# Two token groups share one transposed tile and run their late gate slices together; the sink selection is built by VectorE

## The chip, the cores and the metric

The kernel runs on one core of one Trainium2 chip. A core has TensorE (PE in the profile, with its weight loads shown apart as PEld), VectorE (DVE), ScalarE (ACT), GpSimd (POOL) and SyncE (SP, which here issues DMAs only). The metric is the device time of one execution in microseconds, the median of repeated runs. The profile's own span of one execution (238.3 us) is a little shorter than the device time (240.77 us), since it counts from the first profiled instruction to the last.

## The reference, cut to what matters

Attention with four sink tokens and a window of 128, over 4 batches, 8 heads, 768 positions and head size 64, is followed by a gated feed-forward block over the 3072 tokens it gives:

```python
scores = scale * np.matmul(q, k.transpose(0, 1, 3, 2))
keep = is_sink | in_window            # k < 4, or 0 <= q - k < 128
a = softmax(where(keep, scores, -1e9))
x = (a @ v) with heads joined         # 3072 x 512
g = x @ w_gate                        # 512 x 1536
silu = g * (1.0 / (1.0 + np.exp(-g)))
out = silu * (x @ w_val) @ w_out      # 1536 x 512
```

## The kernel before, in words

**Groups and blocks.** Attention is done in twelve groups of 256 tokens (`g`, three to a batch). The feed-forward block is done in token blocks `tb` of the sizes in `SIZES`: three of 256 tokens (groups 0, 1 and 2), four of 512, and one of 256. For each block the attention output `xn` (tokens on partitions) is transposed into `xT` (model dimension on partitions), in `step_X` (L379): for groups 0, 1, 2 and 4 by TensorE (`px`, L393) and a copy from PSUM (L396 on ScalarE, L400 on VectorE), for the others by a DMA transpose (L388).

**A gate unit.** `gate_a` (L419) projects `xT` with a slice of 128 columns of w_gate into a PSUM bank `pg` (L414) and takes a Tanh on ScalarE into `th` (L428). `gate_b` (L431) projects with w_val into `pv`, and VectorE forms `u = (th + 1) * pg` (L434) and `ht = u * pv` (L435), which is twice the gated value; the factor one half comes with the output copy. A bank holds 512 columns. So for a block of 512 tokens a unit covers one of the twelve slices `f` with four matmuls of 512 columns per projection, and for a block of 256 tokens it covers two slices with eight matmuls of 256 columns. `down` (L453) multiplies `ht` with w_out (L466), 12 matmuls for 128 tokens, copies on ScalarE (L471) and stores through SyncE (L474).

**Order.** Everything is put in order by hand: each engine runs its instructions in the order in which the program lists them, and waits on semaphores where data or a buffer isn't ready. `weave` (L504) goes through a list of units `us` and puts attention steps of later groups into each unit, between its gate projection and its value projection, at the slots given. VectorE work of attention collected in `later` comes after the unit's own `u` and `ht` when `flush` runs. The first list (L634) holds the units of blocks 0 and 1 interleaved (indices 0 to 11), then those of block 2, then the output units of all three. `both` (index 3) starts two units, one of each group, before it finishes either; `alone` (index 2) holds only the transposes of group 1.

**The sinks.** For queries in groups with `c > 0` the four sink keys lie outside the group's own window tiles. Their exponentials `es` (L324) are multiplied with `vsb` (L335), in which a row for each head and sink holds that sink's value in the column block of its head and zero elsewhere. `vsb` for a batch is the sink values (`vcf` for batch 0) times a selection `diag_h` (L270). The selection is made from `th8`, an iota made early (L195): for each of four places q and four heads h, one where `0 <= th8 < 4`, and then joined over q. Before the change GpSimd makes it at L593 to L598 in seven operations: less than, greater or equal, their product, three additions, and a cast. Then GpSimd makes `vsb` for batch 0 (L270) and goes on to issue loads: `nat` (k and q of group 2, L111), further weight slices (L133) and `va` (v, L122). GpSimd's loads before that point, in order, are those of group 1's rows, v of groups 0 and 1, and the first slices of w_gate and w_val.

**Buffers.** `xT` has three buffers in turn, `ht` two; all PSUM tiles share eight banks in turn (`bank`, L78). Blocks 0 and 1 share one `ht` tile, each with a half of it (L425), but each has its own `xT` tile.

Of the kernel before, what the change touches and what calls it, by code (L numbers as in the profile page):

```python
# [8 lines left out]
BF16 = mybir.dt.bfloat16  # L9
AF = mybir.ActivationFunctionType  # L10
ALU = mybir.AluOpType
# [3 lines left out]
def kernel(  # L15
# [12 lines left out]
    nc = tc.nc  # L28
    P = 128
    B, H, S, D = q.shape  # L30
    NS = int(n_sink)
# [5 lines left out]
    DMC = DM // P  # L37
    DFC = DF // P
# [3 lines left out]
    SIZES = [256, 256, 256, 512, 512, 512, 512, 256]  # L42
# [10 lines left out]
    def pool(name, bufs, psum=False):  # L53
        if psum:
            return ctx.enter_context(
                tc.tile_pool(name=name, bufs=bufs, space=bass.MemoryType.PSUM))
        return ctx.enter_context(tc.tile_pool(name=name, bufs=bufs))
# [11 lines left out]
    xtp = pool("xtp", 3)  # L69
# [8 lines left out]
    def bank(shape, dtype, name):  # L78
        return psum.tile(shape, dtype, tag="b", name=name)
# [67 lines left out]
    diag_h = const.tile([P, 4], BF16)  # L147
# [4 lines left out]
    th8 = const.tile([P, 4, 4], FP32)  # L152
    lt8 = const.tile([P, 4, 4], FP32)
# [53 lines left out]
    kTs, qTs, es_t, e_t, xns, xTs = {}, {}, {}, {}, {}, {}  # L207
# [60 lines left out]
    def step_vsb(b):  # L268
        vsb = const.tile([P, 4, D + 1], BF16, tag=f"vsb{b}", name="vsb")
        (nc.vector if b else nc.gpsimd).tensor_tensor(  # L270
            vsb,
            (vcl[:, b - 1:b] if b else vcf).broadcast_to([P, 4, D + 1]),
            diag_h.rearrange("q (h o) -> q h o", o=1).broadcast_to([P, 4, D + 1]),
            op=ALU.mult)
        vsbs.append(vsb)
# [100 lines left out]
    def dense(t, c, n):  # L376
        return t[:, 0:c * n].rearrange("p (c n) -> p c n", c=c)

    def step_X(g, j, evict="v"):  # L379
        t0 = g * 256 + j * P  # L380
        tb = max(i for i in range(len(SIZES)) if OFF[i] <= t0)
        off = t0 - OFF[tb]
        if off == 0:
            xTs[tb] = dense(xtp.tile([P, DMC * 512], BF16, tag="xT", name="xT"),
                            DMC, SIZES[tb])
        if g not in PEX:
            def sp():
                nc.sync.dma_start_transpose(xTs[tb][:, :, off:off + P], xns[g, j])  # L388
            later.append(sp)
            return  # L390
        pt = bank([P, DMC, P], BF16, "px")
        for i in range(DMC):
            nc.tensor.transpose(pt[:, i], xns[g, j][:, i * P:(i + 1) * P], ident)  # L393

        if evict == "a":
            nc.scalar.copy(out=xTs[tb][:, :, off:off + P], in_=pt)  # L396
            return

        def dve():
            nc.vector.tensor_copy(out=xTs[tb][:, :, off:off + P], in_=pt)  # L400
        if evict == "now":
            dve()
        else:
            later.append(dve)

    hts = {}

    def project(ws, tb, f, name):
        n = SIZES[tb]
        ps = bank([P, 512], FP32, name)  # L410
        for i in range(512 // n):
            fi, fo = FOF[f + i]
            for c in range(DMC):
                nc.tensor.matmul(  # L414
                    ps[:, i * n:(i + 1) * n], ws[fi][:, c, fo * P:(fo + 1) * P],
                    xTs[tb][:, c], start=(c == 0), stop=(c == DMC - 1))
        return ps

    def gate_a(tb, f):  # L419
        n = SIZES[tb]  # L420
        if tb not in hts:
            t = hpool.tile([P, DFC * 512], BF16, tag="ht", name="ht")
            hts[tb] = dense(t, DFC, n)
            if tb == 0:
                hts[1] = t[:, DFC * n:2 * DFC * n].rearrange("p (c n) -> p c n", c=DFC)  # L425
        pg = project(wgs, tb, f, "pg")
        th = tpool.tile([P, 512], FP32, tag="th", name="th")
        nc.scalar.activation(th, pg, AF.Tanh, scale=0.5)  # L428
        return pg, th

    def gate_b(tb, f, pg, th):  # L431
        pv = project(wvs, tb, f, "pv")
        u = upool.tile([P, 512], BF16, tag="u", name="u")
        nc.vector.scalar_tensor_tensor(u, th, 1.0, pg, op0=ALU.add, op1=ALU.mult)  # L434
        nc.vector.tensor_tensor(  # L435
            hts[tb][:, f:f + 512 // SIZES[tb]].rearrange("p a n -> p (a n)"), u, pv,
            op=ALU.mult)

    def gate(tb, f, attn):
        a = gate_a(tb, f)  # L440
        for step in attn:
            step()
        gate_b(tb, f, *a)
        flush()

    def both(one_, two_, attn):

        a = [gate_a(*x) for x in (one_, two_)]
        for x, y in zip((one_, two_), a):
            gate_b(*x, *y)  # L450
        flush()
# [28 lines left out]
    def gates(tb):  # L480
        return [(gate, tb, f) for f in range(0, DFC, 512 // SIZES[tb])]

    def downs(tb):
        return [(down, tb, t) for t in range(SIZES[tb] // P)]
# [13 lines left out]
    def Xs(g):  # L498
        return [A(step_X, g, j) for j in range(2)]
# [66 lines left out]
    def pair_mask(p):  # L566
        e = e_t[0][:, 2 * p:2 * p + 2, P:512]
        m = mask0.rearrange("q (o a) x -> q o (a x)", o=1)[:, :, P:512]
        nc.vector.tensor_tensor(e, e, m.broadcast_to([P, 2, 384]), op=ALU.mult)
# [20 lines left out]
    pair_S(3, 2)  # L590
    for p in range(1, NP2):
        pair_mask(p)
    nc.gpsimd.tensor_scalar(lt8, th8, float(NS), None, op0=ALU.is_lt)  # L593
    nc.gpsimd.tensor_scalar(th8, th8, 0.0, None, op0=ALU.is_ge)
    nc.gpsimd.tensor_tensor(lt8, lt8, th8, op=ALU.mult)
    for a, b in ((0, 1), (2, 3), (0, 2)):
        nc.gpsimd.tensor_tensor(lt8[:, a], lt8[:, a], lt8[:, b], op=ALU.add)  # L597
    nc.gpsimd.tensor_copy(out=diag_h, in_=lt8[:, 0])  # L598
    step_vsb(0)
    load_nat(2)  # L600
    load_gate(3)
# [3 lines left out]
    for i in range(4):  # L605
# [13 lines left out]
    masks1 = list(later)  # L619
    later.clear()  # L620
    step_X(0, 0)
    step_X(0, 1)
    flush()
    step_S(1, 1)
# [7 lines left out]

    g0, g1, g2 = gates(0), gates(1), gates(2)
    us = [g0[0], g0[1], (alone, 0, 0), (both, g0[2][1:], g1[0][1:]), g1[1],  # L634
          g1[2], g0[3], g1[3], g0[4], g1[4], g0[5], g1[5],
          *g2, *downs(0), *downs(1), *downs(2)]

    def L(*fs):
# [78 lines left out]
```

## Time and profile before

| what | value |
|---|---|
| device time, median of 3 runs | 240.77 us (240.72 to 241.28) |
| profiled span | 238.3 us |
| PE busy | 231.4 us, 1949 matmuls |
| VectorE, ScalarE, GpSimd busy | 157.7, 114.8, 77.7 us |
| gate and value projections, 256 columns | 192 matmuls each, 24.9 and 24.8 us busy |
| gate and value projections, 512 columns | 192 matmuls each, 49.3 and 49.4 us busy |
| GpSimd's selection, L593 to L598 | 14.32 to 17.38 us of the span |
| GpSimd's vsb, L270 | 1.07 us, from 17.46 us |
| granted TensorE clock | 0.998 of full |

How to read it: the span is cut into busy time by engine, into groups of equal instructions, and into a chain of work that ended last, which goes back from the last instruction to whatever released each step. A line of a timeline gives start and length in us, engine, line of the program, operation, output and inputs, shape and count; in brackets stands how long the engine sat idle before it and what ended the wait. Matmuls are pipelined, so the length of one (273 ns for 256 columns, 379 for 512) is a latency; what a stream of them costs is read from the distance of their starts, or from the pieces of the chain.

### The profile page before, as it was taken

What the parts mean: (1) busy time and instruction counts of PE and PEld (TensorE: products, weight loads), DVE (VectorE), ACT (ScalarE), POOL (GpSimd) and SP (SyncE); (2) the same over time, 40 slices, a digit from 0 to 9 for tenths busy, and PEclk for the clock granted to TensorE, in tenths of its full rate; (3) what the DMA queues carried; (4) which work ended last, traced back from release to release, by engine and by line L of the source; (5) the groups of instructions that cost most, each with busy time, mean ns of one, the idle gap of its engine ahead of it and who ended that gap; (6) DMA issues with size and microseconds to landing.
All of it is one profiled execution on the core that took longest, in us unless ns stands there. A gap on an engine that the chain in (4) does not pass through costs nothing.

```text
span 238.3 us, 5012 instructions
## 1 busy us (share of the span) xinstructions
PE 231.4 (97%) x1949; PEld 132.7 (56%) x1949; DVE 157.7 (66%) x332; ACT 114.8 (48%) x237; POOL 77.7 (33%) x105
## 2 busy tenths in 40 slices
PE   8898999999999999999999999999999999999994
PEld 5576978895454444444445444445444445488443
DVE  4788778668742798970788990588970598877000
ACT  5895485566552845512755622556622663333221
POOL 8989965621707117080080800080000000000000
PEclk9999999999999999999999999999999999999999
DMA  8999999996999999999999994899504200200132
GB/s 144 154 183 166 162 200 208 160 154 76 129 117 207 164 136 105 141 90 200 176 101 120 129 60 134 122 111 133 69 9 132 81 0 3 44 0 4 47 129 88
DMA packets 107655, 27.36 MB, mean 115 GB/s; under 512 B 94704, under 2 KB 104688, under 8 KB 107632
## 3 DMA queue, kind: packets, MB, share of 16 engines
q0 software_dynamic: 76640, 13.90, 82.0%
q1 hardware_dynamic: 30448, 12.89, 29.4%
q8 instruction: 15, 0.25, 0.4%
q10 hardware_dynamic: 544, 0.26, 0.4%
q14 instruction: 8, 0.07, 0.1%
HBM read 28.34 MB, written 6.29 MB: 145 GB/s over the span
## 4 chain that ended last, share of the span: by engine, by line
PE 83%; POOL 7%; DVE 3%; DMA 3%; issue 1%; ACT 1%; SPq 0%; POOLq 0%; DVEq 0%; ACTq 0%
PE pv L414 26%; PE pg L414 25%; PE pd L466 22%; PE o L355 4%; PE s L292 4%; DMA xT<-xn 3%; POOL va L122 1%; POOL rows L100 1%; POOL wv L133 1%; DVE xn L369 1%; PE o L335 1%; PE pn L245 1%; POOL x L188 1%; POOL lt L597 1%; DVE ht L435 1%
## 5 line engine op out<-in xcount | busy, mean ns | idle before, releaser
L414 PE MATMUL pg<-xT,wg 128*128 128x256 bf16 (+1 forms) x384 | 74.2, 326 | 0.8 <-DVE xT L400 0.4
L434 DVE SCALAR_TENSOR_TENSOR u<-th,pg 128x512 bf16<-128x512 f32 x72 | 49.1, 682 | 38.9 <-ACT th L428 38.9
L414 PE MATMUL pv<-xT,wv 128*128 128x256 bf16 (+1 forms) x384 | 74.2, 326 | 0.3 <-ACT e L299 0.2
L428 ACT ACTIVATE th<-pg 128x512 f32<-128x512 f32 x72 | 43.4, 603 | 63.2 <-PE pg L414 62.7
L466 PE MATMUL pd<-wo,ht 128*128 128x512 bf16 (+2 forms) x300 | 65.7, 371 | 0.0
L435 DVE TENSOR_TENSOR ht<-u,pv 128x512 bf16<-128x512 bf16 x72 | 49.5, 687 | 11.7 <-PE pv L414 5.3
L414 PEld LDWEIGHTS <-wg 128*128 128x128 bf16 x384 | 37.3, 98 | 26.7 <-issue 1.1
L414 PEld LDWEIGHTS <-wv 128*128 128x128 bf16 x384 | 34.4, 98 | 19.7 <-issue 1.7
L466 PEld LDWEIGHTS <-ht 128*128 128x128 bf16 x300 | 27.9, 98 | 30.0 <-issue 0.5
L299 ACT ACTIVATE e<-s 128x512 bf16<-128x512 f32 (+1 forms) x88 | 42.7, 580 | 3.5 <-PE s L292 3.5
L111 POOL DMA_DIRECT2D nat<-in_k_dram x20 | 17.7, 888 | 77.2 <-DMA qT<-nat 73.7
L471 ACT ACTIVATE ot<-pd 128x512 f32<-128x512 f32 (+1 forms) x24 | 14.3, 596 | 47.4 <-PE pd L466 47.4
L304 DVE TENSOR_TENSOR e<-e,mask 128x1024 bf16<-128x1024 bf16 (+1 forms) x44 | 27.2, 650 | 4.2 <-ACT e L299 4.2
L122 POOL DMA_DIRECT2D va<-in_v_dram x24 | 21.6, 923 | 2.7 <-DMA wo<-in_moe_w_out_dram 2.5
L369 DVE TENSOR_TENSOR xn<-o,rcp 128x256 bf16<-128x256 f32 x44 | 18.7, 424 | 1.5
L355 PEld LDWEIGHTS <-e 128*128 128x128 bf16 x352 | 15.0, 98 | 7.7 <-issue 0.3
L111 POOL DMA_DIRECT2D nat<-in_q_dram x20 | 17.7, 895 | 0.5 <-DMA wv<-in_moe_w_val_dram 0.4
L355 PE MATMUL o<-va,e 128*128 128x65 bf16 x352 | 17.0, 193 | 0.2 <-DMA va<-in_v_dram 0.2
L292 PE MATMUL s<-qT,kT 64*128 64x128 bf16 (+1 forms) x240 | 12.9, 237 | 0.0
L292 PEld LDWEIGHTS <-kT 64*128 64x128 bf16 x240 | 7.7, 94 | 7.1 <-issue 6.6
L363 DVE RECIPROCAL rcp<-o 128x4 f32<-128x4 f32 x48 | 8.2, 174 | 2.7 <-PE o L355 2.6
L473 DVE TENSOR_SCALAR ot<-pd 128x128 f32<-128x128 f32 x1 | 0.3, 291 | 14.3 <-PE pd L466 14.3
(74 smaller groups left out, 92.3 us busy)
## 6 DMA issues: line engine op xcount, KB each, us to landing
out_dram<-ot SPq DMA_DIRECT2D x23, 256.0 KB
va<-in_v_dram POOLq DMA_DIRECT2D x24, 128.0 KB, 6.6
nat<-in_k_dram POOLq DMA_DIRECT2D x20, 128.0 KB, 4.3
nat<-in_q_dram POOLq DMA_DIRECT2D x20, 128.0 KB, 5.7
wg<-in_moe_w_gate_dram POOLq DMA_DIRECT2D x6, 256.0 KB, 7.2
wv<-in_moe_w_val_dram POOLq DMA_DIRECT2D x6, 256.0 KB, 8.1
wo<-in_moe_w_out_dram POOLq DMA_DIRECT2D x4, 384.0 KB, 11.4
st<-in_q_dram ACTq DMA_DIRECT2D x2, 128.0 KB
```

The costliest lines, as they stand in the source:

```text
L111: nc.gpsimd.dma_start(x[:, i, j].rearrange("p (h d) -> p h d", d=D), src[b, :, t0:t0 + P].rearrange("h p d -> p h d"))
L122: nc.gpsimd.dma_start(va[:, j, :, 0:D], v[b, :, t0:t0 + P].rearrange("h p d -> p h d"))
L292: nc.tensor.matmul(pss[2 * pp + h][:, col:col + n], kTs[b][r, p, kk:kk + P], qTs[b][r, p, qq:qq + n], start=True, stop=True)
L299: nc.scalar.activation(e_t[g][:, h0 + h, lo:512], pss[2 * pp + h][:, lo:512], AF.Exp, scale=scale)
L304: nc.vector.tensor_tensor(e, e, m[:, :, lo:512].broadcast_to([P, 2, 512 - lo]), op=ALU.mult)
L355: nc.tensor.matmul(o, l, r, start=(c == 0 and i == 0), stop=(i == len(mms) - 1), skip_group_check=True)
L369: nc.vector.tensor_tensor(xn, po[:, :, 0:D], rcp.broadcast_to([P, 4, D]), op=ALU.mult)
L414: nc.tensor.matmul(ps[:, i * n:(i + 1) * n], ws[fi][:, c, fo * P:(fo + 1) * P], xTs[tb][:, c], start=(c == 0), stop=(c == DMC - 1))
L428: nc.scalar.activation(th, pg, AF.Tanh, scale=0.5)
L434: nc.vector.scalar_tensor_tensor(u, th, 1.0, pg, op0=ALU.add, op1=ALU.mult)
L435: nc.vector.tensor_tensor(hts[tb][:, f:f + 512 // SIZES[tb]].rearrange("p a n -> p (a n)"), u, pv, op=ALU.mult)
L466: nc.tensor.matmul(po, hts[tb][:, f, ts * P:(ts + 1) * P], wos[f // n][:, f % n, lo:hi], start=(f == 0), stop=(f == DFC - 1))
```

## The change

The transposed outputs of groups 0 and 1 are put in one tile of 512 columns per chunk, the first half for group 0 and the second for group 1. `xTs[0]` and `xTs[1]` are views of the halves, and `xTs["01"]` is the whole. The first six slices of each group stay units of 256 tokens, since group 1's attention isn't done when group 0's units begin. Slices 6 to 11 become six units over both groups together, each one slice wide and 512 tokens long, with half as many matmuls of twice the width. Their `ht` is written into the two halves of the shared `ht` tile by one VectorE operation. The list of units keeps its length, so every attention step keeps its slot.

Apart from this the sink selection `diag_h` is made by VectorE in three operations instead of GpSimd's seven: a less-than, a fused greater-or-equal and product, and a maximum over the places q. It is there to relieve GpSimd, whose queue also issues loads. `vsb` for batch 0 stays on GpSimd.

```diff
-        if off == 0:
+        if tb == 0 and off == 0:
+            xTs["01"] = xtp.tile([P, DMC, 512], BF16, tag="xT", name="xT")
+            xTs[0], xTs[1] = (xTs["01"][:, :, 256 * i:256 * (i + 1)] for i in range(2))
+        elif tb > 1 and off == 0:
             xTs[tb] = dense(xtp.tile([P, DMC * 512], BF16, tag="xT", name="xT"),
                             DMC, SIZES[tb])
...
     def project(ws, tb, f, name):
-        n = SIZES[tb]
+        n = xTs[tb].shape[2]
...
             if tb == 0:
+                hts["01"] = t.rearrange("p (b c n) -> p b c n", b=2, c=DFC)
                 hts[1] = t[:, DFC * n:2 * DFC * n].rearrange("p (c n) -> p c n", c=DFC)
...
         nc.vector.scalar_tensor_tensor(u, th, 1.0, pg, op0=ALU.add, op1=ALU.mult)
+        if tb == "01":
+            nc.vector.tensor_tensor(
+                hts[tb][:, :, f], *(x.rearrange("p (b n) -> p b n", b=2) for x in (u, pv)),
+                op=ALU.mult)
+            return
...
-    nc.gpsimd.tensor_scalar(lt8, th8, float(NS), None, op0=ALU.is_lt)
-    nc.gpsimd.tensor_scalar(th8, th8, 0.0, None, op0=ALU.is_ge)
-    nc.gpsimd.tensor_tensor(lt8, lt8, th8, op=ALU.mult)
-    for a, b in ((0, 1), (2, 3), (0, 2)):
-        nc.gpsimd.tensor_tensor(lt8[:, a], lt8[:, a], lt8[:, b], op=ALU.add)
-    nc.gpsimd.tensor_copy(out=diag_h, in_=lt8[:, 0])
+    nc.vector.tensor_scalar(lt8, th8, float(NS), None, op0=ALU.is_lt)
+    nc.vector.scalar_tensor_tensor(lt8, th8, 0.0, lt8, op0=ALU.is_ge, op1=ALU.mult)
+    nc.vector.tensor_reduce(diag_h, lt8.rearrange("p q h -> p h q"), mybir.AxisListType.X,
+                            op=ALU.max)
...
     us = [g0[0], g0[1], (alone, 0, 0), (both, g0[2][1:], g1[0][1:]), g1[1],
-          g1[2], g0[3], g1[3], g0[4], g1[4], g0[5], g1[5],
+          g1[2], *((gate, "01", f) for f in range(6, DFC)),
           *g2, *downs(0), *downs(1), *downs(2)]
```

More of the change, by code (lines that the diff above doesn't have):

```diff
@@ L419, in gate_a @@
     def gate_a(tb, f):
-        n = SIZES[tb]
         if tb not in hts:
+            n = SIZES[tb]
             t = hpool.tile([P, DFC * 512], BF16, tag="ht", name="ht")
```

## The prediction

> **What bounds the kernel now.** First the page's table of busy time and its chain of work that ended last:
>
> ```profile
> PE 231.4 (97%) x1949; PEld 132.7 (56%) x1949; DVE 157.7 (66%) x332; ACT 114.8 (48%) x237; POOL 77.7 (33%) x105
> ...
> PE 83%; POOL 7%; DVE 3%; DMA 3%; issue 1%; ACT 1%; SPq 0%; POOLq 0%; DVEq 0%; ACTq 0%
> ```
>
> TensorE (PE) is busy for 231.4 of 238.3 us. An edit helps only if it shortens PE's stream or one of PE's few stalls. The 7% of the chain on GpSimd (POOL) lies in the first 19 us. Second, the chain between 14 and 30 us (start, length, what):
>
> ```profile
> 15.57 0.73 POOL lt L597 x2
> ...
> 17.46 1.08 POOL vsb L270
> 18.53 0.04 issue
> 18.57 0.29 PE o L335 x4
> 18.87 1.09 PE o L355 x32
> 19.96 0.02 issue
> 19.98 0.26 DVE rcp L363 x2
> ...
> 21.94 0.69 DVE ht L435
> 22.63 0.34 DVE xT L400
> 22.97 0.05 issue
> 23.02 1.05 PE pg L414 x8
> ```
>
> The sink selection (lt, L593 to L598) leads to vsb, vsb to PE's sink matmuls, and these, through VectorE, to the first gate matmul of group 1 at 23.02. Third, the timeline of the same place, for who waits how long:
>
> ```profile
> 18.03 0.09 PEld L335 LDWEIGHTS <-es 32*128 32x128 bf16 x1 [0.30 <-ACT es L324]
> ...
> 18.57 0.29 PE L335 MATMUL o<-vsb,es 32*128 32x260 bf16 x4 [0.56 <-POOL vsb L270]
> ...
> 18.75 0.69 DVE L435 TENSOR_TENSOR ht<-u,pv 128x512 bf16<-128x512 bf16 x1
> ...
> 19.50 0.18 DVE L363 RECIPROCAL rcp<-o 128x4 f32<-128x4 f32 x1
> ...
> 19.98 0.25 DVE L363 RECIPROCAL rcp<-o 128x4 f32<-128x4 f32 x2 [0.30 <-PE o L355]
> ```
>
> PE loses 0.56 us to vsb; but a second wait ends close behind, for ScalarE's es at 17.98, and VectorE has only 0.30 us of idle time to give back. Fourth, the chain near the end, where 512-token units (four matmuls) turn into 256-token units (eight):
>
> ```profile
> 208.31 0.86 PE pv L414 x4
> 209.17 0.87 PE pg L414 x8
> ```
>
> A projection takes about 0.01 us less as four wide matmuls.
>
> **What the Trainium skill says.** "TensorE: Matmul & The Clock Gate", section "Back-to-back issue gap": a warm matmul of N columns follows the one before after about N/2.4 + 2.5 ns, 216 ns for 512 and 109 ns for 256. The trace agrees: nine projections of four from 201.40 to 209.17 are 0.863 us each (215.8 ns a matmul), twelve of eight from 209.17 to 219.65 are 0.873 us (109.2 ns). So the weight loads that the wide form saves are not what is paid; the few ns per matmul are. "GPSIMD Engine Reference", "3.1 Elementwise": elementwise work costs GpSimd more per element and passes two software dispatches. The trace agrees: 16 elements cost it 0.26 to 0.48 us, and 128x260 cost 1.066 us against VectorE's 0.430 for the same vsb. "DMA: Bandwidth & Descriptors", "Issuing engines are not separate DMA queues": all issuers share the same 16 engines, and issuing from more of them saves only issue time. The trace agrees: GpSimd's loads land one behind another (below).
>
> **Part 1, twelve projections widened.** Six units of (f pair, 256 tokens) become six of (one f, 512 tokens). Columns, Tanh count, u and ht count are the same; ht is written as two runs of 256 and I cost that at nothing, since VectorE's row for it is 687 ns at the same element count and PE in that stretch shows no wait for it (24 to 44 us: PE busy 20.00 of 20.00). Gain: 12 x 0.010 = 0.12 us on PE. One is lost: at 44.14 the gate of group 2 waits for ScalarE's xT copy, a chain that starts at the last unit's pg, so its quicker pv only waits longer. Left: 0.11 us. The weights are needed no sooner: f = 6, 7 come from one slice, as the pair did.
>
> **Part 2, the shared tile.** Both groups' xT lie in one tile. In the changed order of instructions the waits of the gates of group 0 still name only group 0's two copies, and those of group 1 only group 1's, so no false wait arises. The first gate matmul takes a bank that the third exponential (end 14.87) frees, where it waited for the copy ending 14.77: 0.1 us later. The second pg waits for weights that land at 16.92 and is followed by the wait for es; this hides all but 0.05. Later tiles of xT rotate through three buffers that are long free. Cost on the end: 0.
>
> **Part 3, the selection on VectorE.** GpSimd loses seven operations, from 14.32 to 17.38 (3.1 us with their gaps). VectorE gains three. None of these forms with 16 elements is in the trace: the nearest rows are 0.14 us (sk, 128x1) and 0.17 us (rcp, 128x4) at the low end, 0.33 (mask, 128x256) at the high, so 0.45 to 1.0 us; I take 0.6 with the waits between. They stand after the fourth mask product, ended 10.38, and the next reciprocal starts 11.68, after VectorE idled 1.22 us for PE. Hidden at both ends. vsb's new wait for VectorE is over at about 11.0, when GpSimd is still issuing loads; the loads queued behind vsb don't suffer. Its input th is made at 7.5.
>
> vsb then runs 14.3 to 15.4. PE's sink matmuls are next held by es: weight load at 18.03, matmul near 18.10 rather than 18.57, 0.47 us earlier. What becomes of it: PV ends near 19.47. The value projection that follows needs its weights, whose landing events end at 19.90; PE started it at 19.95. So PE waits there instead, and that edge does not move. VectorE does gain: its first reciprocal stays at 19.50 (behind ht, which hangs on ScalarE), but the next two needn't wait until 19.98; they follow at 19.68. The rest, xn, rcp, xn, u, ht, xT, runs on without a gap, 0.30 us sooner, and ends 22.66. Its other inputs allow that: the pv that ht needs ends at 21.00, the transposes behind xT at 21.75. PE reaches group 1's gate after its last group 0 gate at 22.46, so it starts at 22.72 instead of 23.02. Gain: 0.30 us, bounded by 0 (if something else holds xT) and 0.55 (PE's whole wait of 23.02 against 22.46).
>
> The earlier loads: nat starts to issue at 15.4 instead of 18.47. But loads land without a break: 17.75, 18.59, 19.90, 21.30, 22.61, then nat 23.46, 24.29, about 0.85 us per 128 KB and 1.3 per 256 KB, and the page's first nine slices (53 us) move 144 to 208 GB/s with engines nine tenths busy or more. An earlier place in a full queue brings nothing sooner; besides, each load waits for the eighth before it to land. Gain: 0.
>
> Sum: 0.11 + 0.30 = 0.41 us. 240.77 - 0.41 = 240.36, say 240.4.
>
> **Rivals.**
> (a) The gain is given back. PE waits 0.31 us at 112.64 for a DMA transpose:
>
> ```profile
> 112.64 0.59 PE L414 MATMUL pg<-xT,wg 128*128 128x512 bf16 x2 [0.31 <-DMA xT<-xn]
> ```
>
> The loads of nat and their transposes release each other, so they run on a clock of their own, set since the full first 53 us, and the loads that xT shares engines with don't move with PE. If xT lands at the same moment, the 0.41 becomes wait, and 240.7 results. Against it: the transposes are issued behind an output store that follows PE, so at least part moves along.
> (b) A larger gain: the earlier issue does pull the loads forward by a microsecond, which removes the waits at 112.64 (0.31) and perhaps that at 44.14 (0.28): 240.4 - 0.6 = 239.8. Against it: the unbroken landings.
> (c) Slower: GpSimd now writes loads while the weights needed at 19.95, 21.59 and 23.90 are still in flight. If they are served in turn instead of in order, one 128 KB load (0.85 us) comes in ahead of the value weights, which have no slack: 240.77 + 0.85 - 0.11 = 241.5. Against it: landings so far are in order of issue, and their pace was the same with and without issuing beside them.
>
> **How the numbers follow.** Forecast 0.5, (a) 0.2, (b) 0.16, (c) 0.14. The likeliest gives 240.4. The three times of before spread over 0.56 us. The range takes (a) whole, most of (b) and the nearer part of (c), with that spread: 239.5 to 241.3. 0.3% is 0.72 us. The forecast and (a) are within it, unless a DMA landing shifts by chance; (b) at 239.8 passes it, (c) at 241.5 just does. That gives faster 0.27, same 0.57, slower 0.16.
>
> **What would show it.** L270 on GpSimd starting near 14.3 and no wait of PE for it; the three new VectorE operations between 10.4 and 11.7, under 1 us; PE's sink matmuls near 18.1 with the wait for es alone; the value projection still starting at 19.9 to 20.0, now with a wait for wv; group 1's first gate near 22.7; six pairs of four wide matmuls, 0.863 us each; the wait at about 112 between 0.3 and 0.7 us. It would be wrong if weights landed at other moments than 16.92, 19.90, 21.30 and 22.61, if the early lead were swallowed near 112, or if the transposes there came in at another moment altogether.

## The result, and the profile after

| | before | after |
|---|---|---|
| device time, median | 240.82 us (240.43 to 241.53, 6 runs) | 239.05 us (238.85 to 239.57, 6 runs) |
| ratio, with its 95% interval | | 0.9924 (0.9906 to 0.9942) |
| profiled span | 238.3 us | 237.3 us |
| PE busy | 231.4 us, 1949 matmuls | 229.4 us, 1874 matmuls in the trace, which lacks 27 of 1901 |

The changed kernel is 1.8 us faster; 0.4 was forecast, and the time lies below the range. Two more sets of runs of it gave 238.99 and 239.24 us. Of the runs in this document, those of before above 242.85 us and those at 242.25 (e2), 243.57 and 245.31 (e7) and 242.06 us (e18) had a granted clock of 0.984 to 0.993 where all others had 0.997 or more, and the ratios leave out runs over 1.5% above the fastest of their kernel. The profiled execution of before took 240.08 us, 0.7 less than its median, so the two spans differ by 1.0 only.

First, the page of the changed kernel, busy time and the chain by engine:

```profile
PE 229.4 (97%) x1874; PEld 127.3 (54%) x1901; DVE 157.9 (67%) x335; ACT 114.5 (48%) x237; POOL 74.5 (31%) x98
...
PE 88%; ACT 5%; DVE 2%; issue 1%; DMA 1%; SPq 0%; DVEq 0%; ACTq 0%
```

GpSimd, 7% of the chain before, is gone from it; ScalarE has 5%. The chain between 10 and 24 us shows what took its place:

```profile
10.41 0.39 DVE lt L602
10.80 0.02 issue
10.82 0.18 DVE lt L603
11.01 0.02 issue
11.03 0.18 DVE diag_h L604
...
19.55 1.75 ACT xn L366 x8
21.30 0.05 issue
21.35 0.23 PE px L396
21.58 0.87 PE pg L417 x8
22.45 0.00 issue
22.45 1.05 PE pg L417 x8
```

The three VectorE operations end at 11.21. Group 1's first gate matmul starts at 22.45 (23.02 before), straight after group 0's gate: PE waits for nothing there. Then single lines from the timeline of the changed kernel, from several places:

```profile
14.25 0.62 POOL L270 TENSOR_TENSOR vsb<-vcf,diag_h 128x260 bf16<-128x260 f32 x1
18.01 0.10 PEld L335 LDWEIGHTS <-es 32*128 32x128 bf16 x4 [0.28 <-ACT es L324]
19.34 0.33 DVE L363 RECIPROCAL rcp<-o 128x4 f32<-128x4 f32 x3
19.76 1.05 PE L417 MATMUL pv<-xT,wv 128*128 128x256 bf16 x8 [0.38 <-DMA wv<-in_moe_w_val_dram]
21.37 0.69 DVE L444 TENSOR_TENSOR ht<-u,pv 128x512 bf16<-128x512 bf16 x1
43.54 1.03 PE L417 MATMUL pg<-xT,wg 128*128 128x256 bf16 x8
75.65 1.03 PE L417 MATMUL pg<-xT,wg 128*128 128x512 bf16 x4
111.66 1.02 PE L417 MATMUL pg<-xT,wg 128*128 128x512 bf16 x4
```

The last three lines are the first gates of blocks 2, 3 and 4. Before they started at 44.14, 76.25 and 112.64. Between the landmarks the two profiled executions compare so:

| stretch of PE | before | after | difference |
|---|---|---|---|
| start to group 1's first gate | 23.02 | 22.45 | 0.57 |
| to block 2's first gate (all widened units) | 21.12 | 21.09 | 0.03 |
| to block 3's | 32.11 | 32.11 | 0.00 |
| to block 4's | 36.39 | 36.01 | 0.38 |

The last row has the wait of 0.31 us for a transposed xT, now gone: the line at 111.66 has no bracket (e12, below, does this stretch in 35.90, so about 0.1 us may be left). From block 4 on nothing differs by more than 0.1 us. This explains 1.0 us of one execution. That the medians differ by 1.8 is a question of how long PE waits in an ordinary execution of before, which one trace doesn't tell.

### The profile page after: what moved, and what is told of

It reads as the page before. It is cut to its first block, busy times and chain, and to the rows that moved or that the text cites. A ratio compares the mean times of both kernels' runs of the same rounds, so it can differ in the third digit from the quotient of the medians.

```text
span 237.3 us, 4886 instructions
## 1 busy us (share of the span) xinstructions
PE 229.4 (97%) x1874; PEld 127.3 (54%) x1901; DVE 157.9 (67%) x335; ACT 114.5 (48%) x237; POOL 74.5 (31%) x98
## 4 chain that ended last, share of the span: by engine, by line
PE 88%; ACT 5%; DVE 2%; issue 1%; DMA 1%; SPq 0%; DVEq 0%; ACTq 0%
PE pd L475 26%; PE pv L417 26%; PE pg L417 25%; PE o L355 4%; PE s L292 4%; ACT e L299 2%; DMA st<-in_k_dram 1%; ACT e L572 1%; PE pn L245 1%; ACT xn L366 1%; PE o L335 1%; PE pk L320 1%; ACT th L432 1%; DVE u L438 1%; PE px L396 0%
## 5 line engine op out<-in xcount | busy, mean ns | idle before, releaser
L417 PE MATMUL pv<-xT,wv 128*128 128x512 bf16 (+1 forms) x351 | 73.0, 336 | 0.9 <-DMA wv<-in_moe_w_val_dram 0.4
L417 PE MATMUL pg<-xT,wg 128*128 128x512 bf16 (+1 forms) x351 | 73.1, 335 | 0.7
L475 PE MATMUL pd<-wo,ht 128*128 128x512 bf16 (+2 forms) x291 | 64.8, 370 | 0.4
L444 DVE TENSOR_TENSOR ht<-u,pv 128x512 bf16<-128x512 bf16 x66 | 45.4, 688 | 10.4 <-PE pv L417 3.5
L417 PEld LDWEIGHTS <-wg 128*128 128x128 bf16 x360 | 35.0, 98 | 28.2 <-issue 0.9
L417 PEld LDWEIGHTS <-wv 128*128 128x128 bf16 x360 | 32.0, 98 | 21.1 <-issue 1.7
```

The costliest lines, as they stand in the source:

```text
L417: nc.tensor.matmul(ps[:, i * n:(i + 1) * n], ws[fi][:, c, fo * P:(fo + 1) * P], xTs[tb][:, c], start=(c == 0), stop=(c == DMC - 1))
L444: nc.vector.tensor_tensor(hts[tb][:, f:f + 512 // SIZES[tb]].rearrange("p a n -> p (a n)"), u, pv, op=ALU.mult)
L475: nc.tensor.matmul(po, hts[tb][:, f, ts * P:(ts + 1) * P], wos[f // n][:, f % n, lo:hi], start=(f == 0), stop=(f == DFC - 1))
```

## The experiments

Two theories went into the runs. A: PE's path got shorter by more than forecast. B: waits of PE for DMA transposes of xT, at about 77 us (block 3) and 112 us (block 4), vary from execution to execution, and the change removes them. In the expectations A is W and B is D; L says that the earlier loads count, U that the wide units do, F and N that the place of PE's instruction fetches does or doesn't; E and C are the opposites of D and F that stand with them. Ratios are against before on the same chip; 0.001 is 0.24 us.

**Each part alone, and the loads held back.** e1 is the kernel before under another label. e2 has the selection alone, e3 the wide units alone. e4 is the changed kernel in which GpSimd does its seven operations as well, into tiles that nobody reads, between vsb and the loads, so that the loads start as late as before:

```diff
+    nc.gpsimd.tensor_scalar(lt9, th8, float(NS), None, op0=ALU.is_lt)
+    nc.gpsimd.tensor_scalar(th9, th8, 0.0, None, op0=ALU.is_ge)
...
+    nc.gpsimd.tensor_copy(out=dg9, in_=lt9[:, 0])
```

> The kernel before, unchanged, for a second profile of it. Both theories: 240.8 us, ratio 1.000. What is looked for: whether the wait for the transposed tile at about 112 us of the span (0.31 us in the first profile) and the moment at which the loads of nat for group 8 are issued (102.38 us) come back the same. If the chain of loads and transposes runs on a clock of its own that varies, they differ by half a microsecond or more while PE up to 100 us does not; if it is tied to PE, they come back within 0.1 us.

> Only the sink selection moves to VectorE; the units of the first two groups stay as before. Theory W (PE's wait for vsb, and what follows it up to group 1's first gate, 0.57 us in the profile after, is what counts, the rest is units and chance): 240.2 us, ratio 0.9975. Theory L (the loads that GpSimd issues 3 us earlier pull the chain of loads and transposes forward, so that later waits of PE for transposed tiles shrink too): 239.2 us, ratio 0.993. Theory U (the wide units bring over 1 us): 240.5 us, ratio 0.999.

> Only the shared tile and the six wide units; the selection stays on GpSimd with its seven operations. Theories W and L: 240.7 us, ratio 0.9995 (twelve projections quicker by 0.01 us). Theory U: 239.6 us, ratio 0.995.

> The changed kernel, with the seven GpSimd operations of the old selection put behind vsb and ahead of the loads of group 2, on tiles that nobody reads: vsb stays early, the loads are issued about when they were before. Nothing of the computation changes. Theory W: as the changed kernel, 239.1 us, ratio to before 0.993. Theory L: the part that the early loads bring is lost, 240.1 us, ratio 0.997. Theory U: 239.1 us.

| kernel | median (range, runs), us | ratio (95%) |
|---|---|---|
| e1 | 240.79 (239.78 to 243.52, 22) | 0.9987 (0.9966 to 1.0008) |
| e2 | 240.28 (239.22 to 242.25, 22) | 0.9964 (0.9943 to 0.9985) |
| e3 | 240.28 (239.49 to 241.52, 22) | 0.9973 (0.9955 to 0.9992) |
| e4 | 239.67 (238.67 to 240.40, 12) | 0.9935 (0.9911 to 0.9959) |

Both parts gain, -0.87 and -0.65 us by their ratios, -1.5 together. e2 is as W had it; e3 lies between W and U, e4 between W and L. The wide units alone bring six times what their matmuls can save, so something other than matmul time is in play. The ranges say what: at the full clock each set of before spreads over 2.3 to 3.3 us, the changed kernel over 0.9 in all its 19 runs. In the timeline of e1 PE waits where the first trace of before had no wait (before first, then e1):

```profile
76.25 1.03 PE L414 MATMUL pg<-xT,wg 128*128 128x512 bf16 x4
...
77.05 1.02 PE L414 MATMUL pg<-xT,wg 128*128 128x512 bf16 x4 [0.46 <-DMA xT<-xn]
```

Other traces have other draws of this wait: 1.53 us in e2, 1.25 in e15, 0.31 in e16, and 0.48 at 112 us in e4. The three traces of the changed kernel (after, e9, e14) have none.

**The waits taken away on PE.** In e5 (before), e6 (selection alone), e7 (units alone) and e8 (the changed kernel) the xT of groups 3 and 6 is transposed by TensorE, so PE no longer waits for a DMA there, at the price of PE's own work:

```diff
-    PEX = (0, 1, 2, 4)
+    PEX = (0, 1, 2, 3, 4, 6)
...
-        ((19, 19, 19, 20), PVs(3)), (20, Xs(3)),
+        ((19, 19, 19, 20), PVs(3)), (21, Xs(3)),
```

> The kernel before, with the transposes of groups 3 and 6 done by TensorE (as those of groups 0, 1, 2 and 4 are) instead of by DMA, so that PE has no DMA transpose left to wait for at about 77 and 112 us of the span. It costs PE 16 transposes (0.9 us). Theory D (the time of before is a floor near 239.7 us plus waits for those transposes, which vary from run to run): about 240.6 us at every run, spread under 0.6 us instead of 4 us. Theory E (those waits are incidental, the spread has another source): 241.2 + 0.9 = 242.1 us with the same spread.

> The selection on VectorE alone, with the same two groups of transposes on TensorE. Theory D: the gain at PE's wait for vsb is kept in full, 0.5 to 0.6 us less than the kernel before with that edit. Theory E: 0.9 us less, as without the edit (0.9964).

> The wide units alone, with the same two groups of transposes on TensorE. Theory D: 0.05 to 0.15 us less than the kernel before with that edit, since the units' own gain on PE is that small and what came on top in the first run of the units alone (0.65 us) was fewer DMA waits. Theory E: 0.65 us less.

> The changed kernel with the same two groups of transposes on TensorE. Theory D: 0.6 to 0.75 us less than the kernel before with that edit, the sum of the two parts; the rest of the measured 1.8 us is then waits for transposes that the change makes shorter. Theory E: 1.5 to 1.8 us less.

| kernel | median (range, runs), us | against e5 |
|---|---|---|
| e5 | 241.28 (241.09 to 241.49, 14) | |
| e6 | 240.70 (240.23 to 241.22, 22) | -0.58 |
| e7 | 241.28 (241.08 to 245.31, 22) | 0.00 |
| e8 | 240.58 (240.03 to 241.16, 22) | -0.70 |

The unmodified before, run beside them, took 239.57 to 243.47 us (67 runs); e5 stays within 0.4, and so do all runs of e7 at the full clock. None of the four traces has a wait for a transpose. So these two transposes are where most of before's spread is from. The level of e5 isn't D's 240.6: the transposes on PE cost more than the 0.9 us expected, 1.2 us by the ratios and 1.7 by the medians against e12 below, where the waits are gone without them. And what the change does to PE's own path is seen without them: -0.58 us for the selection, nothing for the units, -0.70 for both. That is A, and it is not 1.8.

**The waits taken away in SyncE's queue.** SyncE issues all DMA transposes in program order, and group 3's xT stands behind the k and q transposes of group 5, which wait for loads. In e12 (before) and e11 (the changed kernel) group 3's xT transposes go ahead of group 5's. So that the last transpose of groups 6, 8 and 10 also gets ahead of an output store, one attention step of these groups moves up by one unit; this is part of the edit. e9 and e10 are the changed kernel and e4 once more, beside them:

```diff
-        (15, [A(xbar, 4)]), (15, [NV(5)]), (19, [A(xbar, 5)]), (19, [NV(6)]),
+        (15, [A(xbar, 4)]), (15, [NV(5)]), (19, [NV(6)]),
...
-        ((19, 19, 19, 20), PVs(3)), (20, Xs(3)),
+        ((19, 19, 19, 20), PVs(3)), (20, Xs(3) + [A(xbar, 5)]),
...
-                ((12, 12, 13, 13) if s else (10, 10, 11, 12), PVs(gb)),
-                ((14, 14) if s else (12, 13), Xs(gb))]
+                ((12, 12, 13, 13) if s else (10, 10, 11, 11), PVs(gb)),
+                ((14, 14) if s else (12, 12), Xs(gb))]
```

> The changed kernel, unchanged, with more runs than the first time. Theory D: a floor at 238.8 us and waits for the DMA transposes on top that vary from run to run; the first median (239.05 us of 6 runs) was on the lucky side, so 239.4 us, ratio 0.994 to 0.996. Theory L (the loads issued earlier shorten the waits for the transposes by a whole microsecond): 239.1 us, ratio 0.992.

> The changed kernel with GpSimd's loads for group 2 onwards held back by the old seven operations, again, now on the chip of the changed kernel. Theory D: as the changed kernel within 0.2 us. Theory L: 0.5 us or more above it.

> The changed kernel; SyncE's queue alone in another order: group 3's transposes ahead of the transposes of k and q for group 5 (whose loads they wait for), and the last transpose of groups 6, 8 and 10 ahead of the output store that stood before it. To that end one attention step of these groups moves up by one unit. Theory D: the waits at 77 and 112 us go, median 238.9 us, spread under 0.8 us. If the waits come from engines shared with the loads and not from the order of the queue: as the changed kernel.

> The kernel before with the same order of SyncE's queue. Theory D: 239.7 us, spread under 0.8 us, so 1.3 us less than the kernel before and 0.7 us more than the changed kernel in that order. If the waits come from the shared engines: as the kernel before, 241.0 us.

| kernel | median (range, runs), us | ratio (95%) |
|---|---|---|
| e9 | 238.99 (238.68 to 239.23, 6) | 0.9926 (0.9899 to 0.9953) |
| e10 | 239.26 (238.60 to 240.35, 13) | 0.9944 (0.9924 to 0.9964) |
| e11 | 239.04 (238.63 to 239.27, 7) | 0.9932 (0.9908 to 0.9956) |
| e12 | 239.60 (239.48 to 240.01, 12) | 0.9951 (0.9933 to 0.9969) |

In e12 the timeline has group 3's xT issued at 65.10 (71.32 in before) and both gates without a wait:

```profile
65.10 3.25 SPq L388 DMA_TRANSPOSE xT<-xn  x2
...
76.22 1.03 PE L414 MATMUL pg<-xT,wg 128*128 128x512 bf16 x4
...
112.12 1.03 PE L414 MATMUL pg<-xT,wg 128*128 128x512 bf16 x4
```

The other order gives before 1.0 to 1.2 us (medians 240.58 and 239.60; ratio 0.9951), and gives the changed kernel nothing (e11 against e9). The difference left is e12 to e11, 0.56 us, close to e8's 0.70. So the 1.8 us are about 0.6 of PE's path and about 1.2 of waits that the change removed without touching a transpose. e9 came out as L had it, not D: the first time of the changed kernel was no luck. e10 lies between the two. Holding the loads back costs 0.27 us by the medians and 0.43 by the ratios (e10 against e9, intervals overlapping), and 0.26 by the ratios in e4 against the first set; e4 and e10 spread over 1.7 us again. So the early loads have a part in removing the waits, well under half of those 1.2.

**What removes the rest of the waits: the place of PE's instructions, and with it that of their fetches.** The traces have a DMA queue for instructions. It carries 15 packets of 16 KB (0.25 MB on the page), which the profile counts on the same 16 engines as loads and transposes. That they are PE's program is read from their moving with PE's instructions, as follows. The six wide units need 48 matmuls and 48 weight loads fewer, so every later fetch comes at another place: after the third (at about 31 us in both) they start at 41.7, 52.9, 65.9, 82.9 us in before, and at 45.3, 56.4, 69.4, 85.3 in the changed kernel. e13 keeps the rest of the change and puts the instructions back: each matmul of the wide units is issued as two of 256 columns. e15 does the same to e3. e14 and e16 repeat the changed kernel and e3 beside them. e17 adds the same 96 instructions to the changed kernel, but in the last block of 512 tokens, from 184 us on (the second cut, against e13):

```diff
-            for c in range(DMC):
-                nc.tensor.matmul(
-                    ps[:, i * n:(i + 1) * n], ws[fi][:, c, fo * P:(fo + 1) * P],
-                    xTs[tb][:, c], start=(c == 0), stop=(c == DMC - 1))
+            halves = 2 if tb == "01" else 1
+            m = n // halves
+            for h in range(halves):
+                for c in range(DMC):
+                    nc.tensor.matmul(
+                        ps[:, i * n + h * m:i * n + (h + 1) * m],
+                        ws[fi][:, c, fo * P:(fo + 1) * P],
+                        xTs[tb][:, c, h * m:(h + 1) * m],
+                        start=(c == 0), stop=(c == DMC - 1))
```

```diff
-            halves = 2 if tb == "01" else 1
+            halves = 2 if tb == 6 and f < 6 else 1
```

> The changed kernel, its six wide units kept in shape, but each matmul of 512 columns issued as two of 256 with the weights loaded again: PE's program has as many instructions as before the change, and its fetches of instructions fall where they fell before. Theory F (the fetches' place against the loads makes or spares the waits for transposes): the waits come back, median 239.6 to 240.2 us, spread of 2 us. Theory N (it has no part): 239.1 us, 0.1 us for the narrow matmuls, spread as the changed kernel's 0.6 us.

> The changed kernel, unchanged, as the reference on this chip. Both theories: 239.0 us, spread of 0.6 us.

> The wide units alone (selection on GpSimd), each matmul issued as two of 256 columns. Theory F: as the kernel before, 240.6 to 241.0 us. Theory N: as the units alone, 240.3 us.

> The wide units alone, unchanged, as the reference on this chip. Both theories: 240.3 us, ratio 0.997 to 0.998. If what they brought the first time was chance: 240.7 us.

> The changed kernel; as many extra PE instructions as in e13 (48 matmuls with their weight loads), but in six units of the last 512-token block, behind 186 us: the fetches before 112 us stay where they are in the changed kernel. Theory F (place): 239.2 us, spread of 0.6 us, the 0.1 us for the narrow matmuls included. Theory C (the count as such): as e13, 240.1 us, spread of 2 us or more.

> e13's kernel with SyncE's queue in the order of e11, which took the waits at 77 and 112 us from the kernel before. If e13's spread lies in these waits: 239.1 to 239.3 us, spread under 0.8 us. If the fetches delay PE in another way too: 239.6 us or more.

| kernel | median (range, runs), us | ratio (95%) |
|---|---|---|
| e13, changed, narrow | 240.09 (238.63 to 242.76, 22) | 0.9964 (0.9944 to 0.9985) |
| e14, changed | 239.24 (238.92 to 239.53, 7) | 0.9932 (0.9905 to 0.9959) |
| e15, units, narrow | 240.66 (239.73 to 241.83, 14) | 0.9992 (0.9970 to 1.0014) |
| e16, units | 240.45 (239.47 to 241.16, 22) | 0.9980 (0.9965 to 0.9995) |
| e17, changed, narrow late | 238.99 (238.75 to 239.97, 14) | 0.9946 (0.9928 to 0.9963) |
| e18, e13 with e11's order | 239.19 (238.65 to 242.06, 22) | 0.9941 (0.9923 to 0.9960) |

e13 is 0.85 us slower than e14 by the medians, though the intervals of the ratios overlap, and spreads over 4 us, like before or more; twelve projections of eight instead of four cost 0.12 us at most. e17 has as many instructions as e13 and a short median, with a spread of 1.2 us where 0.6 was expected; its ratio lies between those of e13 and e14. So it isn't the number of instructions that counts, but where they stand. With that the fetches move: they start at 41.3, 51.7 and 66.7 us in e13, at 44.8, 56.1 and 68.7 in e17. No run moved the fetches and nothing else. e18 has e13's instructions with the xT transposes issued first, and its median is back at 239.19: most of what the place costs goes through these transposes. But for the run at 242.06, its runs end at 240.11. The profiled one (240.05) has no wait for a transpose; it is late from the start: its third gate projection begins at 22.56 (21.42 in after), behind 0.51 us of waiting for weights. e15 against e16 (0.21 us) shows little: without the selection the wide units still meet waits, 0.31 us at 77 us in the profile of e16 and 1.25 in that of e15.

How a fetch can get at the transposes is seen on SyncE and GpSimd. In the timeline of e13:

```profile
55.40 1.22 SPq L259 DMA_TRANSPOSE qT<-nat  x1
58.40 1.75 POOL L111 DMA_DIRECT2D nat<-in_k_dram  x2 [8.93 <-DMA qT<-nat]
66.46 1.96 SPq L259 DMA_TRANSPOSE kT<-nat  x1
76.45 1.02 PE L420 MATMUL pg<-xT,wg 128*128 128x512 bf16 x4 [0.46 <-DMA xT<-xn]
```

and in that of e17:

```profile
54.04 1.22 SPq L259 DMA_TRANSPOSE qT<-nat  x1
58.90 1.75 POOL L111 DMA_DIRECT2D nat<-in_k_dram  x2 [10.08 <-DMA qT<-nat]
66.53 1.22 SPq L259 DMA_TRANSPOSE kT<-nat  x1
75.40 1.03 PE L420 MATMUL pg<-xT,wg 128*128 128x512 bf16 x4
```

The bracket on the k load of group 5 says that a transposed q of an earlier group released it. From that transpose's issue to the release pass 3.00 us in e13 and 4.86 in e17. From the k load to the issue of group 5's last q transpose, behind which xT stands, it is the other way round: 10.1 us in e13, 8.9 in e17. The DMA views of the two show a fetch in the long leg of each; e13 from 66.2 to 67.2 us, with group 5's loads (software) in flight and its transposes being issued:

```profile
q0 software_dynamic: 1164, 0.15, 230.7%
q8 instruction: 1, 0.02, 8.3%
```

and e17 from 56 to 57 us, where it has the engines nearly to itself (columns: packets, MB, share of the 16 engines; the times of overlapping packets add up):

```profile
q8 instruction: 1, 0.02, 7.4%
q1 hardware_dynamic: 9, 0.00, 0.4%
```

The same legs in all thirteen profiled executions in which group 3's xT is transposed by DMA and in the old order, read from the timelines, the instruction queue and the landing events (all in us; the last two columns are for the later of group 3's two xT transposes):

| kernel | fetches | last q transpose to k load | k load to group 5's last q transpose | xT of group 3 issued | group 6's k load, from the later xT's issue | later xT, issue to landing |
|---|---|---|---|---|---|---|
| before | 52.9, 65.9 | 3.00 | 10.46 | 71.32 | +0.58 | 2.44 |
| e1 | 53.1, 66.1 | 3.00 | 10.10 | 71.09 | -0.17 | 4.50 |
| e2 | 51.3, 65.6 | 2.99 | 11.55 | 71.65 | -0.16 | 4.04 |
| e13 | 51.7, 66.7 | 3.00 | 10.10 | 70.44 | -0.26 | 4.55 |
| e15 | 52.8, 67.3 | 3.01 | 10.94 | 71.76 | -0.24 | 4.42 |
| e3 | 57.2, 69.8 | 4.50 | 8.83 | 71.42 | +0.22 | 3.72 |
| e16 | 57.3, 69.9 | 4.49 | 8.75 | 71.55 | +0.21 | 3.61 |
| after | 56.4, 69.4 | 4.50 | 9.04 | 69.97 | +0.91 | 2.44 |
| e14 | 56.2, 69.5 | 4.50 | 8.88 | 69.59 | +0.83 | 2.50 |
| e17 | 56.1, 68.7 | 4.86 | 8.94 | 70.26 | +0.22 | 3.61 |
| e9 | 56.2, 69.4 | 2.98 | 9.52 | 68.09 | +0.24 | 5.51 |
| e4 | 56.1, 69.1 | 4.61 | 8.96 | 70.67 | +0.21 | 3.36 |
| e10 | 56.1, 69.3 | 4.01 | 8.17 | 69.28 | +1.55 | 2.52 |

The executions fall in two kinds by the fetches alone, the first five rows and the rest. A fetch within about 2.1 us after the transpose's issue goes with 1.0 to 1.9 us more until the load is released; e9, whose transpose was issued 2.5 us ahead of the fetch, has the short leg. With a fetch at 65.6 to 67.3 the second leg is longer, 10.1 us or more against 9.5 or less. And in twelve of the thirteen, one of SyncE's issues that overlapped the second fetch took longer than its like, a transpose 1.57 to 2.25 us instead of 1.19 to 1.23, or a store 1.02 to 1.52 instead of 0.53 (such long issues occur elsewhere too, 1.99 us at 75.97 in e4).

But these legs don't decide when xT arrives. Its later transpose is issued at 71.77 us in e13, and at 71.71, 71.80 and 71.58 in after, e14 and e17; it lands at 76.32, and at 74.16, 74.30 and 75.19. The kinds differ in the last leg, and that goes with the place of GpSimd's next load. In the timelines of e1 and of after:

```profile
71.09 2.54 SPq L388 DMA_TRANSPOSE xT<-xn  x2
72.24 1.76 POOL L111 DMA_DIRECT2D nat<-in_k_dram  x2 [7.94 <-DMA qT<-nat]
...
69.97 2.96 SPq L391 DMA_TRANSPOSE xT<-xn  x2
72.63 1.75 POOL L111 DMA_DIRECT2D nat<-in_k_dram  x2 [8.38 <-DMA qT<-nat]
```

In the second kind, e9 apart, the second fetch starts 0.8 to 1.9 us after group 5's last q transpose, and group 6's k load, which that transpose releases, starts 3.10 to 3.26 us after the fetch, however long ago the transpose was issued. So this load comes behind the later xT transpose, which then lands after 2.4 to 3.7 us. In the first kind the load comes just ahead, and xT lands after 4.0 to 4.6 us, later than PE needs it. The first trace of before is the exception in its kind: there the load came behind, xT landed in 2.44 us, and PE had no wait at 77. e9's xT took 5.51 us, but was issued 2 us sooner.

The columns are a correlation over thirteen executions. What was tried is the place of the instructions (e13, e17) and the order of the transposes (e11, e12, e18); no run moved group 6's load alone. Why one 16 KB packet holds up the release of a load by more than its own microsecond is not shown, and part of the second leg can be due to the output store issued at 59 to 60 us, which in the first kind comes a microsecond after the k load and in most of the second right beside it.

## Why the prediction was wrong, step by step

**The step that failed** is the sum: it knew PE's own path alone and put the change of PE's waits for DMA-transposed xT at nothing. The gate of block 3 was taken as free of such waits and the one at 112 as 0.3 to 0.7 us, kept, since one trace showed that, and that trace was an execution 0.7 us quicker than the median. In an ordinary execution of before these two waits cost 1.0 to 1.2 us (e12), and the change makes them all but vanish. "Gain: 0" for the earlier loads is a smaller part of the miss: they bring 0.3 to 0.4 us (e10, e4), though in the trace of after group 5's k load starts at 58.99 against 58.92, the lead of 3 us gone. Rival (b), a larger gain by fewer waits at 112, named one of the two waits, and the loads as the only reason. The larger reason was set aside in the reading of the matmul gap, "the weight loads that the wide form saves are not what is paid": true of PE's time, but where the saved instructions stood made 0.85 us of difference (e13 against e14). That this went through the fetches is argued from the traces.

**Part 3's path was right, its size was not: 0.30 forecast, 0.57 in the trace, 0.58 in e6 against e5.** As forecast, the three operations on VectorE lie between the mask product and the next reciprocal (10.32 to 11.21; 0.81 us of work, where 0.6 was forecast with the waits between), vsb starts at 14.25, the sink matmuls run at 18.01 with the wait for es alone, and the value projection then waits for its weights. The term that was too small is what VectorE gives back. Its first reciprocal was held at 19.50 in the working; it began at 19.34, and three took 0.33 us in one go where before spent 0.18 and 0.25. So ht came at 21.37, not 21.64, the xT copy ended at 22.40, not 22.66, and PE didn't wait at all. The gain is about the upper bound that the prediction gave for PE's whole wait, 0.55. "That edge does not move" failed too, harmlessly: wv landed for a start at 19.76 instead of 19.95.

**Part 1: 0.11 forecast, 0.03 in the trace, 0.00 in e7 against e5.** The Trainium skill's "TensorE: Matmul & The Clock Gate", section "Back-to-back issue gap", gives the prediction's formula for an isolated matmul, and some 131 ns as sustained at 512 columns; the streams of this kernel ran at the formula's pace, 215.8 ns, and the measurement decides. The pure projections do take 0.86 us, as the chain of the changed kernel says:

```profile
38.52 0.86 PE pv L417 x4
...
40.24 0.34 PE px L396 x4
```

But at the changes to other matmuls the gain goes back: px took 0.27 us behind 256-column matmuls and takes 0.34 here. From the first widened pv to the last widened pg pass 10.20 us before (31.85 to 42.05) and 10.18 after (31.27 to 41.45). ht written as two runs takes 688 ns like the others, as said.

**Part 2: 0, and right.** PE's stream through the first gates has no new wait, and group 0's gates end at 22.45 where 22.46 was forecast.

**The rivals (a) and (c)** didn't occur: the lead of 0.60 us at block 3 (76.25 to 75.65) is kept to the end, and no load came in ahead of the value weights.

No run beats the changed kernel by more than its spread. Putting the xT transposes first in the kernel before (e12) gets within 0.6 us of it, without the wide units and the new selection.

## What to carry to other kernels

When repeated runs spread over more than the gain that is looked for, find out first which wait varies: take it off the path (e5, e12) and compare the versions there, because one trace shows one draw of it. In a queue that issues in order, as SyncE's here, a transfer that the critical engine needs soon is better not put behind transfers that still wait for loads (e12). And an edit that changes the number of instructions of an engine moves its instruction fetches among the other transfers (by 3 to 4.5 us here); where transfers are waited for, test such an edit against a copy with the count restored elsewhere (e13, e17) before giving the gain to the edit itself.

## What of the hardware was unexpected

- PE's instruction fetches, 16 KB each, took 0.9 to 2.3 us on the DMA engines. Putting 96 instructions back, which moved the fetches by 3 to 4.5 us, went with 0.85 us in the median, and with a spread of 4 us instead of 0.6.
- From the issue of group 4's last q transpose to the start of the load behind it passed 3.00 us, to within 0.02 us, in six of these executions, and 4.0 to 4.9 us in the seven with a fetch in between.
- The same xT transpose landed 2.4 to 2.5 us after its issue when GpSimd's next load started 0.6 us or more behind it, and 4.0 to 4.6 us after it when that load started just ahead.
- The same vsb operation on GpSimd took 0.62 us in 16 of 20 traces and 1.06 to 1.14 in four. It isn't the change: the kernel before took 1.07 us in its first trace and 0.62 in that of e1.
- Four wide matmuls save 0.01 us over eight of half the width, and in the trace of after the next transposes take 0.07 longer behind them.
